# Two empty places in the gate's tick list, and three changes of order at the experts' beginning, in a fused attention and mixture-of-experts kernel

## Chip, cores, metric

The kernel runs on one core of one Trainium2 chip. The metric is the device time of one execution in microseconds (us). Every launch computes everything from the inputs in DRAM to the output in DRAM.

## The reference

Three stages follow each other: attention that keeps the 32 largest scores of a row, a gated linear layer, and a layer of eight experts of which each token uses one.

```python
scores = scale * q @ k.T                       # 4 batches, 8 heads, 576 x 576, head size 64
kth = np.partition(scores, -32)[..., -32]      # per row
attn = softmax(where(scores >= kth, scores, -1e9)) @ v
x = attn.transpose(0, 2, 1, 3).reshape(2304, 512)
x = ((x @ w_a) * (x @ w_b)) @ w_out            # 512 -> 1536 -> 512, weights in float64
xn, en = x / norm(x), expert_emb / norm(expert_emb)
logits = xn @ en.T / tau
e = argmax(logits); g = softmax(logits)[e]
out = g * (relu(x @ w1[e]) @ w2[e])            # 512 -> 1024 -> 512, per token
```

All products are made of three float32r products of high and low parts, so that each input of a product is first split: high = rounded value, low = value - high.

## The kernel before

**Attention.** 144 blocks of 128 rows, one per step. A step's work goes through the engines in this order: TensorE makes two score halves (L373), ScalarE copies them out (L374, tile `s`, 5 buffers), VectorE finds the 32nd largest value with four MAX8 and three MATCH_REPLACE8 (L394, L397) and writes a bias (L399), ScalarE makes a penalty (L406, tile `z`), GpSimd subtracts it (L409), ScalarE takes the exponential with its row sum (L411), TensorE turns the block (L428). After the last block of a part, GpSimd adds a small number to the row sums (L437, tile `rc`) and VectorE takes their reciprocal (L439) in the middle of its top-k work. In this stage the order of TensorE, VectorE, ScalarE and GpSimd is that in which the Python code issues the instructions. Each engine executes its own list in order.

**Gated layer in the background.** `moe1` is a generator. It works on 9 groups of 256 tokens; each has 12 blocks f of 128 hidden columns. `background` advances it between the attention's instructions, one `yield` at a time. For a block f TensorE makes the two products a and b (24 matmuls, L729), ScalarE copies them out (L743, tile `gab`, 2 buffers), GpSimd multiplies them (`gab<-gab`), ScalarE makes the high part (`gh`), GpSimd the low part (`gl<-gab,gh`). Two blocks later (`LAG` = 2) TensorE uses `gl` and `gh` for the second product (`second`, L676). The three small operations are not issued at once: they are entries of a list `pend`, from which `tick()` takes one at a time (all three then show as L663, the line of `tick`). A block has seven ticks: three in the a product, two in the b product, two in `second`. Before, the list of a block is: product, empty, high part, low part. `second(f)` empties what is left of f's entries before it issues its matmuls. When attention has ended (about 836 us), the remaining groups run alone; the routing of tokens to experts is made beside them.

**Experts.** From here only TensorE's order is that of the code; the other engines' orders come from a scheduler. `first_expert` does 256 rows of one expert early, `last_tile` its last 80 rows, and the loop over e = 1..7 the other experts. The rows are gathered by GpSimd's indirect DMA (`pick`, L1132), turned by TensorE (`turn_x`, L1145) and split by ScalarE (L1148) and VectorE (L1149) into `xT`. Weights come in units of 1 MB (`raw`, 2 buffers, L1093), and each unit is split into `u` (4 buffers) in two halves: ScalarE L1099, VectorE L1100, some 1.05 and 1.22 us for a half. `upto(n)` issues units up to n. A `gate` is a ScalarE copy of one column (L1096) that writes into the unit's first half and reads a tile named by `gate[0]`: that half can't be converted before that tile is written. In `last_tile` L1288 are the matmuls of the first product, L1291 its ReLU, L1295 the turning of its result, L1298 and L1299 its split into `hT`, L1181 the second product. In the loop `stage1` is the first product (L1169, ReLU L1173, low part L1174), and L1342 the second.

Of the kernel before, what the change touches and what calls it, by code (L numbers as in the profile page):

```python
# [87 lines left out]
def fused_kernel(  # L88
# [25 lines left out]
    NE, _, F2 = w1.shape  # L114
# [3 lines left out]
    NF2 = F2 // P  # L118
# [88 lines left out]
    with ExitStack() as ph:  # L207
# [440 lines left out]
        def moe1(G):  # L648

            gi = G.gi  # L650
            g0, N = GROUPS[gi]
            G.inputs()
            xg, ws = G.xg, G.ws
            LA = WB // 2 - 1
            while len(ws) < LA:
                G.load()
            px = [None, None]
            gs = {}
            pend = []

            def tick():
                if pend:
                    pend.pop(0)[1]()  # L663

            def second(f, tiles=(0, 1)):
                while pend and pend[0][0] <= f:
                    tick()
                hi, lo = gs[f]
                if gi == 0:
                    conv.need(2, f)  # L670
                for t in tiles:
                    ts = slice(t * P, (t + 1) * P)
                    if f == 0:
                        px[t] = mp.tile([P, DM], F32, name="x1", bufs=2)
                    for i, (g, w) in enumerate(((lo, 0), (hi, 1), (hi, 0))):
                        pe.matmul(  # L676
                            px[t], g[:, ts], wo[:, w, f], start=(f == 0 and i == 0), stop=(f == NF - 1 and i == 2)
                        )
                    if f == NF - 1:
                        r = route(g0 // P + t, px[t])  # L680
                        next(r)
                        routes.append(r)
                        debt[1] = 0.0
                    tick()
                    yield 0.64

            begun = {}
            if gi == 0:
                for f in range(2):
                    while not (conv.ready(0, f) and conv.ready(1, f)):  # L690
                        yield None
                    begun[f] = [mp.tile([P, 512], F32, name=nm, bufs=2)[:, :256] for nm in ("ab", "x1")]
                    for i in range(2):
                        wt = conv.tiles[i, f]
                        for c in range(KC - 1):
                            for a, x in TERMS1:
                                pe.matmul(
                                    begun[f][i],
                                    wt[:, a, c, :],
                                    xg[x][:, c, :],  # L700
                                    start=(c == 0 and (a, x) == TERMS1[0]),
                                    stop=False,
                                )
                            yield 3 * N / 2400
                while ready[0] < N:
                    yield None

            for f in range(NF):
                nxt = todo[1][1] if len(todo) > 1 and todo[1][0] <= now[0] else None
                if f >= (NF - 4 if gi else NF - 1) and nxt:  # L710
                    nxt.inputs()
                if f + LA < NF:
                    G.load()
                elif nxt:
                    nxt.load()
                if gi == 0:
                    conv.begun = f
                    while now[0] < NRW and not (conv.ready(0, f) and conv.ready(1, f)):
                        yield None
                    for i in range(2):  # L720
                        conv.need(i, f)
                    ws[f] = [conv.tiles[i, f] for i in range(2)]
                ab = mk.tile([P, 2, GN], F32, name="gab")
                p = None if f in begun else mp.tile([P, 2, 256], F32, name="ab", bufs=2)
                ps_ = begun[f] if f in begun else [p[:, 0], p[:, 1]]
                for i, wt in enumerate(ws[f]):
                    terms = [(a, x, c) for (a, x) in TERMS1 for c in range(KC) if f not in begun or c == KC - 1]
                    for j, (a, x, c) in enumerate(terms):
                        pe.matmul(  # L729
                            ps_[i],  # L730
                            wt[:, a, c, :],
                            xg[x][:, c, :],
                            start=(j == 0 and f not in begun),
                            stop=(j == len(terms) - 1),
                        )
                        if j % 4 == 3 and (i == 0 or j < 11):
                            tick()
                            yield 4 * N / 2400
                if f in begun:
                    for i in range(2):  # L740
                        act.activation(ab[:, i], ps_[i], AF.Copy)
                else:
                    act.activation(ab, p, AF.Copy)  # L743
                recent[0] = ab
                yield 4 * N / 2400
                hi = mk.tile([P, GN], F32R, name="gh", bufs=LAG + 2)
                lo = mk.tile([P, GN], F32R, name="gl", bufs=LAG + 2)
                gs[f] = hi, lo
                pend.append((f, partial(pool.tensor_tensor, ab[:, 0], ab[:, 0], ab[:, 1], op=OP.mult)))
                pend.append((f, lambda: None))  # L750
                pend.append((f, partial(act.activation, hi, ab[:, 0], AF.Copy)))
                pend.append((f, partial(pool.tensor_tensor, lo, ab[:, 0], hi.bitcast(F32), op=OP.subtract)))
                if f >= LAG:
                    yield from second(f - LAG)
            tail[0] = tail[0] if gi == len(GROUPS) - 1 else lambda: None
            nxt = todo[1] if len(todo) > 1 and todo[1][0] <= now[0] and todo[1][1].ws else None
            if nxt:
                nxt[2] = moe1(nxt[1])
            for tiles in ((0,), (1,)) if gi == len(GROUPS) - 1 else ((0, 1),):
                for f in range(NF - LAG, NF):  # L760
                    for _ in range(6 if nxt else 0):
                        yield next(nxt[2])
                    for _ in range(NTF if tiles[0] >= ET else 0):
                        tail[0]()
                    yield from second(f, tiles)
# [307 lines left out]
    with ExitStack() as ph:  # L1073
        w2p = ph.enter_context(tc.tile_pool(name="w2p", bufs=2, side="right"))

        gate = [None]
# [194 lines left out]
        def last_tile():  # L1271
# [5 lines left out]
            pick(xs[t], ids[0][:m, t, 0:1])  # L1277
            nx = gather(NE - 1)
            turn_x((xs, xT), t)
            turn_x(nx, 0, NE - 1)  # L1280
            hs = []
            for half in range(2):
                u = units[half]
                p = bank("h")
                n = 0
                for a, b in TERMS:
                    for c in range(KC):
                        pe.matmul(p[:m], xT[b][:, c, t * P :], u[:, a, c, :], start=(n == 0), stop=(n == 11))  # L1288
                        n += 1
                hs.append(result())  # L1290
                act.activation(hs[-1][:m], p[:m], AF.Relu)  # L1291
            for half, h in enumerate(hs):
                pt = bank("tr")
                for j in range(4):
                    pe.transpose(pt[:, j * P : j * P + m], h[:m, j * P : (j + 1) * P], ident[:m, :m])  # L1295
                pv = pt.rearrange("p (j k) -> p j k", j=4)[:, :, :m]
                hi, lo = (y[:, half * 4 : half * 4 + 4] for y in hT)
                act.activation(hi, pv, AF.Copy)  # L1298
                dve.tensor_tensor(lo, pv, hi.bitcast(F32), op=OP.subtract)  # L1299
# [18 lines left out]
        for e in range(1, NE):  # L1318
            r = NE - e
            n, M = caps[r], rows_of(r)  # L1320
            nx = None
# [11 lines left out]
            if e + 1 < NE:  # L1333
                yT = wx.tile([P, KC, cap], F32, name="yT", bufs=1)[:, :, :n]
                for d in range(KC):
                    p = bank("y")[:, :n]
                    for f in range(NF2):
                        if f % 4 == 0 and d == 0:
                            upto(4 * e + 2 + f // 4 + UB)
                        u = units[4 * e + 2 + f // 4]  # L1340
                        for i, (a, b) in enumerate(TERMS):
                            pe.matmul(  # L1342
                                p,
                                u[:, b, f % 4, d * P : (d + 1) * P],
                                hT[a][:, f],
                                start=(f == 0 and i == 0),
                                stop=(f == NF2 - 1 and i == 2),
                            )
                        if f == XF and d:
                            turn_x(nx, d - 1, r - 1)  # L1350
# [95 lines left out]
```

## Time and profile before

| what | value |
|---|---|
| median of 3 runs (lowest, highest) | 1262.11 us (1260.44, 1264.21) |
| the profiled execution | 1259.81 us |
| its span, first to last instruction | 1258.0 us |
| TensorE matmul busy, share of the span | 1139.1 us, 91% |
| VectorE | 917.0 us, 73% |
| ScalarE | 819.5 us, 65% |
| GpSimd | 728.4 us, 58% |
| DMA, mean | 190 GB/s |
| mean granted TensorE clock | 0.967 of 2.4 GHz |

The sums are made against the profiled execution's own time; it lies 2.3 us (0.2%) below the median of the three runs. In the rows further down, "busy" is time in which an engine executed, a number in square brackets is the engine's idle time just before the instruction and the name behind the arrow is what ended it. PEld is TensorE's weight load, which runs beside the matmuls. An engine name with q (POOLq) is its sequencer.

### The profile page before, as it was taken

How to read it: one execution, taken by the hardware profiler on the slowest of the kernel's cores; microseconds unless marked ns; L12 is line 12 of the kernel's file. 1: busy time of each engine (PE TensorE's matmuls, PEld its weight loads, DVE VectorE, ACT ScalarE, POOL GpSimd, SP SyncE). 2: the span in 40 equal slices, each digit the busy share in tenths (PEclk: the TensorE clock that was granted, in tenths of full speed). 3: DMA queues.
4: the chain of work that ended last, by engine and by line, in shares of the span. 5: the costliest groups of instructions: out<-in, count | busy, mean ns of one | idle time of the engine just before them, and what ended most of it. 6: DMA issues, size and time to landing. Idle time of an engine off the chain costs nothing. (4 is left out here: it accounts for less than half of the span.)

```text
span 1258.0 us, 23887 instructions
## 1 busy us (share of the span) xinstructions
PE 1139.1 (91%) x8124; PEld 983.9 (78%) x8125; DVE 917.0 (73%) x2015; ACT 819.5 (65%) x1964; POOL 728.4 (58%) x1195
## 2 busy tenths in 40 slices
PE   5676789988999998999999998989999989999996
PEld 4445567777887887888887887777898868999995
DVE  8999999999999998899999988850110215655540
ACT  5777988887877877777877877653542424545441
POOL 5565787776777876676787776664555420232221
PEclk8788999999999998999999999999999989999999
DMA  7334667666774666667565677656997235465530
GB/s 235 129 113 139 200 213 254 221 214 199 250 226 139 193 208 214 183 202 212 179 189 181 209 198 208 199 146 206 336 288 220 97 123 205 170 209 207 193 101 27
DMA packets 129200, 240.05 MB, mean 191 GB/s; under 512 B 24896, under 2 KB 74176, under 8 KB 129074
## 3 DMA queue, kind: packets, MB, share of 16 engines
q1 hardware_dynamic: 125170, 228.74, 57.6%
q0 software_dynamic: 3904, 9.75, 2.0%
q8 instruction: 65, 1.06, 0.3%
q14 instruction: 61, 0.50, 0.1%
HBM read 198.38 MB, written 40.31 MB: 190 GB/s over the span
## 5 line engine op out<-in xcount | busy, mean ns | idle before, releaser
L394 DVE MAX8 t<-y 128x8 f32<-128x576 f32 x432 | 311.7, 749 | 2.7
L409 POOL TENSOR_TENSOR z<-s,z 128x576 f32<-128x576 f32 x144 | 206.2, 1432 | 49.7 <-ACT z L406 44.3
L397 DVE MATCH_REPLACE8 y<-t,y 128x576 f32<-128x576 f32 x288 | 213.9, 743 | 0.0
L729 PE MATMUL ab<-xg,wab 128*128 128x256 f32 x1398 | 210.5, 290 | 2.2 <-DMA wab<-wab_d 0.9
L729 PEld LDWEIGHTS ab<-xg,wab 128*128 128x128 f32 x1398 | 183.8, 191 | 5.2 <-DMA wab<-wab_d 1.1
L428 PE MATMUL tr<-ident,z 128*128 128x128 f32 x720 | 135.2, 287 | 51.5 <-ACT z L411 47.2
L729 PE MATMUL ab<-raw,wab 128*128 128x256 f32 x1152 | 172.6, 288 | 3.8 <-DMA wab<-wab_d 2.6
L374 ACT ACTIVATE s<-tr 128x288 f32<-128x288 f32 x288 | 118.3, 411 | 72.3 <-POOL z L409 37.3
L729 PEld LDWEIGHTS ab<-raw,wab 128*128 128x128 f32 x1152 | 150.3, 189 | 6.9 <-DMA wab<-wab_d 2.6
L431 ACT ACTIVATE wt<-tr 128x384 f32<-128x384 f32 (+2 forms) x320 | 128.1, 413 | 41.4 <-PE tr L428 40.7
L428 PEld LDWEIGHTS tr<-ident,z 128*128 128x128 f32 x720 | 89.2, 145 | 71.8 <-ACT z L411 60.3
L676 PE MATMUL x<-wo,gh 128*128 128x512 f32 x432 | 136.7, 398 | 0.0
L663 POOL TENSOR_TENSOR gab<-gab 128x256 f32<-128x256 f32 x108 | 81.1, 751 | 90.0 <-ACT gab L743 79.7
L1153 POOL DMA_INDIRECT out_dram<-o,ids x24 | 31.2, 1300 | 174.1 <-ACT o L1152 122.2
L1100 DVE TENSOR_TENSOR u<-raw,u 128x1024 fp32r<-128x1024 f32 x64 | 75.9, 1221 | 73.1 <-ACT u L1099 50.1
L373 PE MATMUL tr<-kT,qT 128*128 128x288 f32 x512 | 123.6, 326 | 4.6 <-ACT s L374 3.5
L663 POOL TENSOR_TENSOR gl<-gab,gh 128x256 fp32r<-128x256 f32 x108 | 83.0, 768 | 59.5 <-ACT gh L663 50.8
L411 ACT ACTIVATE z<-z,bi 128x576 f32<-128x576 f32 x144 | 112.2, 779 | 0.3 <-POOL z L409 0.3
L406 ACT ACTIVATE z<-s,bi 128x576 f32<-128x576 f32 x144 | 111.4, 773 | 0.2 <-DVE bi L399 0.2
L394 DVE MAX8 t<-s 128x8 f32<-128x576 f32 x144 | 107.0, 743 | 5.0 <-ACT s L374 4.8
L397 DVE MATCH_REPLACE8 y<-t,s 128x576 f32<-128x576 f32 x144 | 106.9, 742 | 0.0
L676 PE MATMUL x<-wo,gl 128*128 128x512 f32 x216 | 93.3, 432 | 6.3 <-POOL gl L663 6.2
(201 smaller groups left out, 2240.2 us busy)
## 6 DMA issues: line engine op xcount, KB each, us to landing
wab<-wab_d SPq DMA_DIRECT2D x192, 512.0 KB, 4.5
raw<-in_moe_w_dram SPq DMA_DIRECT2D x28, 1024.0 KB, 5.3
wab_d<-wab SPq DMA_DIRECT2D x24, 512.0 KB, 4.5
kT<-kT_d SPq DMA_DIRECT2D x20, 576.0 KB, 5.8
vs<-in_v_dram SPq DMA_DIRECT2D x36, 256.0 KB, 3.1
kT_d<-kT SPq DMA_DIRECT2D x16, 576.0 KB, 5.0
raw<-in_moe_w_a_dram SPq DMA_DIRECT2D x12, 512.0 KB, 4.4
raw<-in_moe_w_b_dram SPq DMA_DIRECT2D x12, 512.0 KB, 4.3
```

Source lines behind the costliest of these rows:

```text
L373: pe.matmul(p, l, r, start=(i == 0), stop=(i == len(terms) - 1))
L374: act.activation(t.s[:, cs], p, AF.Copy, scale=SCALE)
L394: dve.max(v, cur)
L397: dve.match_replace(out=rest, in_to_replace=v, in_values=cur, imm_value=LOWEST)
L406: act.activation(t.w, t.s, AF.Relu, bias=t.bi[:, 1:2], scale=-HUGE)
L409: pool.tensor_tensor(t.w, t.s, t.w, op=OP.subtract)
L411: act.activation(t.w, t.w, AF.Exp, bias=t.bi[:, 0:1], accum_out=t.o.sm[:, t.slot : t.slot + 1])
L428: pe.transpose(pt[:, i * P : (i + 1) * P], t.w[:, k0 : k0 + P], ident)
L431: act.activation(th[:, sl, w], pv[:, :, src], AF.Copy)
L663: pend.pop(0)[1]()
L676: pe.matmul(px[t], g[:, ts], wo[:, w, f], start=(f == 0 and i == 0), stop=(f == NF - 1 and i == 2))
L729: pe.matmul(ps_[i], wt[:, a, c, :], xg[x][:, c, :], start=(j == 0 and f not in begun), stop=(j == len(terms) - 1),)
```

## The change

Two empty entries are added to the list of a block's small operations: one ahead of the product, one ahead of the low part. The list now has six entries for the block's seven ticks: empty, product, empty, high, empty, low. So the product and the high part are issued one tick later, the low part two ticks later. In `last_tile` the turning of the next expert's first 128 gathered rows is issued behind the first product's matmuls rather than ahead of them. In the loop, a gate is put on the unit that is issued at the start of the second product: its first half waits for the last block of `hT`.

```diff
@@ moe1
                 gs[f] = hi, lo
+                pend.append((f, lambda: None))
                 pend.append((f, partial(pool.tensor_tensor, ab[:, 0], ab[:, 0], ab[:, 1], op=OP.mult)))
                 pend.append((f, lambda: None))
                 pend.append((f, partial(act.activation, hi, ab[:, 0], AF.Copy)))
+                pend.append((f, lambda: None))
                 pend.append((f, partial(pool.tensor_tensor, lo, ab[:, 0], hi.bitcast(F32), op=OP.subtract)))
@@ last_tile
             nx = gather(NE - 1)
             turn_x((xs, xT), t)
-            turn_x(nx, 0, NE - 1)
             hs = []
             for half in range(2):
                 u = units[half]
...
                 hs.append(result())
                 act.activation(hs[-1][:m], p[:m], AF.Relu)
+            turn_x(nx, 0, NE - 1)
             for half, h in enumerate(hs):
@@ the loop over e
                     for f in range(NF2):
                         if f % 4 == 0 and d == 0:
+                            gate[0] = hT[0][:, NF2 - 1, 0:1] if f == 0 else None
                             upto(4 * e + 2 + f // 4 + UB)
```

What this moves, first on GpSimd in the attention stage, around the `rc` of a part that ends near 371 us. Before:

```order
L663 TENSOR_TENSOR gab<-gab 128x256
L408 TENSOR_SCALAR bi<-t_4627 128x1
L409 TENSOR_TENSOR z<-s,z 128x576
L663 TENSOR_TENSOR gl<-gab,gh 128x256
L663 TENSOR_TENSOR gab<-gab 128x256
L408 TENSOR_SCALAR bi<-t_4722 128x1
L409 TENSOR_TENSOR z<-s,z 128x576
L437 TENSOR_SCALAR rc<-sm 128x5
```

and with the change:

```order
L408 TENSOR_SCALAR bi<-t_4626 128x1
L409 TENSOR_TENSOR z<-s,z 128x576
L663 TENSOR_TENSOR gab<-gab 128x256
L663 TENSOR_TENSOR gl<-gab,gh 128x256
L408 TENSOR_SCALAR bi<-t_4722 128x1
L409 TENSOR_TENSOR z<-s,z 128x576
L437 TENSOR_SCALAR rc<-sm 128x5
L663 TENSOR_TENSOR gab<-gab 128x256
```

Each of the two gate products has moved behind the softmax subtraction that followed it, the second one behind the `rc` too. TensorE's and VectorE's orders are the same in the whole attention stage; on ScalarE only the high parts (and a routing instruction) stand later.

Second, TensorE at the experts' beginning (`xT` 80x512 are the 80 last rows of the first expert, `tr<-ident,xg 128x128` the next expert's rows). Before:

```order
L1145 MATMUL tr<-ident,xg 128x80 x4
L1145 MATMUL tr<-ident,xg 128x128 x4
L1288 MATMUL h<-u,xT_14069 80x512 x4
L1288 MATMUL h<-u,xT_14070 80x512 x4
L1288 MATMUL h<-u,xT_14069 80x512 x8
L1288 MATMUL h<-u,xT_14070 80x512 x4
L1288 MATMUL h<-u,xT_14069 80x512 x4
L1295 MATMUL tr<-ident,o 128x80 x8
```

and with the change:

```order
L1147 MATMUL tr<-ident,xg 128x80 x4
L1289 MATMUL h<-u,xT_14069 80x512 x4
L1289 MATMUL h<-u,xT_14070 80x512 x4
L1289 MATMUL h<-u,xT_14069 80x512 x8
L1289 MATMUL h<-u,xT_14070 80x512 x4
L1289 MATMUL h<-u,xT_14069 80x512 x4
L1147 MATMUL tr<-ident,xg 128x128 x4
L1297 MATMUL tr<-ident,o 128x80 x8
```

The four transposes of the next expert's rows have moved behind all 24 matmuls (the changed kernel's line numbers are one to three higher).

Third, ScalarE in the second expert (e = 1), from its first product to its second (`hT` are the ReLUs, `u<-raw 128x1024` halves of weight units). Before:

```order
L1173 ACTIVATE hT_14199<-h 128x264
L1099 ACTIVATE u<-raw 128x1024 x2
L1173 ACTIVATE hT_14199<-h 128x264 x2
L1099 ACTIVATE u<-raw 128x1024 x2
L1173 ACTIVATE hT_14199<-h 128x264 x3
L1099 ACTIVATE u<-raw 128x1024 x2
L1173 ACTIVATE hT_14199<-h 128x264 x2
L1099 ACTIVATE u<-raw 128x1024 x2
```

and with the change:

```order
L1175 ACTIVATE hT_14199<-h 128x264
L1101 ACTIVATE u<-raw 128x1024 x2
L1175 ACTIVATE hT_14199<-h 128x264 x2
L1101 ACTIVATE u<-raw 128x1024 x2
L1175 ACTIVATE hT_14199<-h 128x264 x4
L1101 ACTIVATE u<-raw 128x1024 x2
L1175 ACTIVATE hT_14199<-h 128x264
L1098 ACTIVATE u<-hT_14199 128x1
L1101 ACTIVATE u<-raw 128x1024 x2
```

The seventh ReLU has moved ahead of a unit's two conversions, the eighth still stands behind them, and the gate's copy stands in front of the last two.

## Rows read from the trace of the kernel before

**Rows 1.** Busy time by stretch, with the columns in the first line

```profile
core 0: us, PE busy (x) PEld busy (x) DVE busy (x) ACT busy (x) POOL busy (x), PEclk, DMA share, GB/s
...
200.00:836.00 636.00, 600.26 (x4557) 514.38 (x4556) 592.79 (x1362) 492.12 (x1274) 462.78 (x798) 0.98 0.66 202
...
1024.50:1030.50 6.00, 5.97 (x16) 3.92 (x17) 0.69 (x1) 0.60 (x1) 1.08 (x2) 0.50 0.67 248
1030.50:1041.50 11.00, 10.24 (x53) 6.69 (x52) 6.49 (x8) 6.62 (x11) 0.41 (x1) 0.99 0.16 53
...
1100.00:1258.00 158.00, 147.63 (x1023) 142.34 (x1022) 71.26 (x102) 64.25 (x102) 35.94 (x30) 0.98 0.43 147
```

**Rows 2.** Waits in attention, 200 to 836 us: total us, times, longest

```profile
POOL gab L663 <- ACT gab L743: 55.2, 43, 3.9
...
POOL gl L663 <- ACT gh L663: 36.6, 35, 4.0
...
DVE rc L439 <- POOL rc L437: 25.8, 11, 3.7
...
PE x L676 <- POOL gl L663: 6.2, 3, 3.8
...
PE tr L316 <- POOL qs L229: 5.5, 2, 3.2
...
DVE t L394 <- ACT s L374: 4.0, 2, 2.9
```

**Rows 3.** GpSimd's timeline ahead of two late rc: start us, us, instruction

```profile
368.55 0.74 POOL L663 TENSOR_TENSOR gab<-gab 128x256 f32<-128x256 f32 x1 [2.31 <-ACT gab L743]
...
369.43 1.43 POOL L409 TENSOR_TENSOR z<-s,z 128x576 f32<-128x576 f32 x1
370.94 0.25 POOL L437 TENSOR_SCALAR rc<-sm 128x5 f32<-128x5 f32 x1
...
808.31 0.74 POOL L663 TENSOR_TENSOR gab<-gab 128x256 f32<-128x256 f32 x1 [1.33 <-ACT gab L743]
```

**Rows 4.** VectorE's timeline at three late reciprocals

```profile
322.84 0.18 DVE L439 RECIPROCAL rc<-rc 128x4 f32<-128x4 f32 x1 [2.44 <-POOL rc L437]
...
371.22 0.19 DVE L439 RECIPROCAL rc<-rc 128x5 f32<-128x5 f32 x1 [2.14 <-POOL rc L437]
...
810.97 0.18 DVE L439 RECIPROCAL rc<-rc 128x4 f32<-128x4 f32 x1 [2.26 <-POOL rc L437]
```

**Rows 5.** TensorE and GpSimd at the ends of two groups

```profile
259.72 0.50 PE L676 MATMUL x<-wo,gl 128*128 128x512 f32 x1 [2.10 <-POOL gl L663]
...
259.63 0.40 POOL L227 TENSOR_SCALAR qs<-qr 128x256 fp32r<-128x256 f32 x1
...
478.46 0.80 PE L676 MATMUL x<-wo,gl 128*128 128x512 f32 x1 [3.85 <-POOL gl L663]
```

**Rows 6.** Timeline of the experts' beginning

```profile
1019.88 0.47 PE L1145 MATMUL tr<-ident,xg 80*128 80x80 f32 x4 [0.16 <-DMA xg<-row_d,ids]
...
1020.53 0.44 ACT L1148 ACTIVATE xT<-tr 128x320 fp32r<-128x320 f32 x1
...
1024.53 1.12 PE L1145 MATMUL tr<-ident,xg 128*128 128x128 f32 x4 [4.18 <-DMA xg<-row_d,ids]
...
1025.30 8.23 PE L1288 MATMUL h<-u,xT 128*80 128x512 f32 x24
...
1030.56 2.49 PEld L1288 LDWEIGHTS h<-u,xT 128*80 128x80 f32 x11 [0.18 <-issue]
...
1035.06 0.92 PE L1181 MATMUL y<-u,hT 128*80 128x512 f32 x3 [0.35 <-DVE hT L1299]
```

**Rows 7.** DMA issues, 1017.60 to 1017.95 us: KB each, us to landing

```profile
raw<-in_moe_w_dram SPq DMA_DIRECT2D x1, 1024.0 KB, 5.3
```

**Rows 8.** Timeline in expert e = 1, from first to second product

```profile
1053.92 2.01 ACT L1099 ACTIVATE u<-raw 128x1024 fp32r<-128x1024 f32 x2 [3.00 <-DMA raw<-in_moe_w_dram]
...
1057.77 2.87 PE L1342 MATMUL y<-hT,u 128*128 128x264 f32 x12 [2.20 <-DVE hT L1174]
```

## The prediction

> **What bounds the kernel now.** I read the busy times by stretch, the waits of the attention stage, and then timelines. Over the whole span TensorE is the busiest engine (91%, in the table above), but the two places that the change touches have limits of their own. In attention (200 to 836 us) TensorE is busy for 600.3 and VectorE for 592.8 of 636 us, GpSimd for 462.8 [rows 1]: two engines run nearly full, each with some 40 us of idle time, and neither has much room to wait. The reader should see in the waits that VectorE's are nearly all of one kind: its reciprocal waits 25.8 us, in 11 pieces, for the `rc` that GpSimd makes; for scores, its real input, it waits 4.0 us [rows 2]. GpSimd in turn stands 55.2 us in front of a gate product and 36.6 us in front of a low part, since ScalarE has not made their inputs yet [rows 2]. The two belong together: at 368.55 GpSimd had stood 2.31 us for a gate product, worked 0.74 us on it, and only then came to the softmax subtraction (1.43) and `rc` at 370.94 [rows 3]; VectorE, at its reciprocal, had waited 2.14 us [rows 4].
>
> At the experts' beginning the bound is one gather. TensorE finishes the transposes of the last 80 rows at 1020.35 (1019.88 + 0.47), and then stands 4.18 us for the next expert's rows, although the 24 matmuls that follow need only the copy that ScalarE ends at 1020.97 (1020.53 + 0.44) [rows 6]. The idle time has a second price: from 1024.5 to 1030.5 the granted clock is 0.50, that is 1.2 GHz [rows 1], so the 24 matmuls take 8.23 us, though the last 11 take only 2.49 [rows 6]. From 1100 us on TensorE is busy for 147.6 of 158 us [rows 1], what is missing being the drain at the very end; a gain here is kept.
>
> **The change, part by part.**
>
> *Gate list.* No instruction is added; an empty entry costs nothing on the chip. Matched one by one, the changed order puts 38 of the 72 gate products of this stretch, and 46 of the 72 low parts, behind at least one other GpSimd instruction. GpSimd's idle time just before these 84, from whatever cause, sums to 38.0 + 31.6 = 69.6 us (the two rows have 91.8 for all 144 [rows 2]); the others keep their place. What this saves counts only where VectorE or TensorE stood for GpSimd. Ten `rc` waits are long (2 to 3.7 us, one 0.89). Ahead of seven of them, from the one at 322.84 us to the one at 810.97 [rows 4], a gate operation that stood in front of `rc` now stands behind it. Near 371 us its wait and work are 2.31 + 0.74 = 3.05 us [rows 3], more than the 2.14 that VectorE lost [rows 4]. At 811 us a product (1.33 + 0.74) [rows 3] leaves, and a low part before it, and all 2.26 can go. Counted so for the seven, each capped by VectorE's wait and by how long the subtraction's own input had been there, it makes 0.9 + 2.1 + 1.7 + 0.9 + 2.0 + 1.9 + 2.3 = 11.8 us, the upper bound. The lower bound is a loss: low parts are issued two ticks later. In the middle of a group they are finished 3 to 25 us before TensorE wants them, in most places over 6. But at group ends TensorE already stands for them, 6.2 us in 3 places [rows 2], 2.10 and 3.85 of it in the two longest [rows 5]. At the first of these the changed order puts one small split (0.40) [rows 5] in front of the low part, at the second nothing. Six group ends at 0.5 us make +3 us. Between -11.8 and +3 I take **-7**, some 60% of the upper bound: VectorE runs only 3 us or so behind its scores, so an advance is soon limited by TensorE. That TensorE can follow in part is seen in its own waits for GpSimd, such as 5.5 us for split queries in two places [rows 2]; at one of them a gate product that stood in front leaves.
>
> One rule speaks against that term. The Trainium skill, "Perfetto Trace Analysis", section "Identifying the Most-Contended Engine", says to improve the engine of highest occupancy first; GpSimd is only third here. By that rule the term would be 0 and not -7. The rows side with it on TensorE's occupancy and against it on the waits; it is a rival below.
>
> *Transposes behind the matmuls.* The matmuls can start at about 1021.05, some 0.1 us after ScalarE's copy. Per matmul 2.49 / 11 = 0.226 us at 2.4 GHz [rows 6], so 24 take 5.5 and end at 1026.5. The clock should hold, for the gap is now 0.7 us; the gaps of under 0.5 us between 1030.5 and 1041.5 leave it at 0.99 [rows 1]. The gathered rows have landed by 1024.53, so the four transposes follow at once (0.6) and cover the ReLU of the second half. After them a new chain appears: the second half's transposes use the PSUM bank that the moved ones filled, so they wait for its ScalarE copy (0.60) and VectorE split (0.69), and then for their own copy and split (0.44 and 0.49). The second product then starts near 1029.1 where it started at 1035.06 [rows 6]: **-5.9**. The weight unit that ScalarE splits between the two ReLUs is no obstacle: its load landed 5.3 us after its issue at 1017.7 [rows 7], at 1023.0. Bounds: -6.5 if that chain hides, -3.2 if the clock falls all the same (13 matmuls at 0.2 us more).
>
> *The gate in the loop.* Before, TensorE stands 2.20 us in expert e = 1 for the seventh and eighth block of `hT`, whose ReLUs are behind two conversions on ScalarE that waited 3.00 us for a weight load [rows 8]. With the change the seventh goes ahead, but the eighth still stands behind them, so the wait moves three matmuls back and stays. The load is issued when an earlier unit has been split, and that advances by 5.4 us where TensorE advances by 5.9. What is left is three matmuls fewer at half clock, 0.7, less that 0.5: **-0.2**; bounds +1 and -3.7 (the wait and the slow matmuls behind it all gone). In the other experts the eighth ReLU stood ahead of the gated half already; a copy of 0.2 us each on ScalarE, which is under half busy there [rows 1], costs nothing.
>
> Sum: -7.0 - 5.9 - 0.2 = -13.1 us. On the profiled execution's 1259.8 that is 1246.7; the median of the runs stood 2.3 higher, so the forecast is **1249**.
>
> **Rivals.**
>
> *Attention gives nothing (B).* TensorE is the bound there: the reciprocals come sooner, VectorE then waits for scores instead, and the attention ends when it did. For it: TensorE's 94%, and waits for GpSimd that only change place. Against it: VectorE waits only 4.0 us for scores now [rows 2]. Time: 1262.1 - 6.1 = 1256.
>
> *The beginning gives only a third (C).* The new chain through the PSUM bank, or the gathers, take most of it: -7 - 2 = 1253.
>
> *Little change (D).* The shifted order costs attention 3 to 5 us through high and low parts that come just late, and offsets the experts' gain: 1259 to 1262.
>
> *Slower (E).* At a group's end the last block's low part is now issued only when `second` empties the list, right in front of its matmuls and behind six steps of the next group; TensorE then stands there every time. At six group ends with the longest wait seen, 3.85 [rows 5], it is 23.1 - 6.2 = +16.9, with the experts' -6.1 and nothing else 1273. It decides from 2.7 us a group end on ((6.1 + 3.8 + 6.2) / 6). Against it: at these six ends the low part is moved behind 1, 4, 0, 2, 0 and 1 GpSimd instructions only.
>
> **How the numbers follow.** The forecast has 0.55, B 0.22, C 0.10, D 0.06, E 0.07. A measurement of this kernel tells 0.3%, 3.8 us, from no change. Faster: 0.53 of the forecast, 0.19 of B, 0.09 of C, in all 0.81; same 0.12 (D whole, the edges of the others); slower 0.07 (E). The forecast's own range, attention -3 to -12 and the experts -5 to -6.5, is 1243.6 to 1254; with B and C, and a little beyond at the low end for attention at its bound, the range is 1241 to 1259.
>
> **What would show it.** Right: VectorE's wait for `rc` falls from 25.8 to some 14 us, GpSimd's two waits to some 40; the last reciprocals come about 7 us sooner; L1289 starts within 1 us of the 80-row transposes, at 2.4 GHz; the next second product starts 8 to 9 us after those transposes, not 14.7. Wrong: an attention stage of the same length with VectorE's waits for scores grown (B), a wait of over 2 us in front of the moved transposes or of L1297 (C), or TensorE's waits for `gl` well over 6.2 us (E).

## The result and the profile after

| | before | changed |
|---|---|---|
| median (runs, lowest to highest) | 1262.82 us (6, 1260.44 to 1264.21) | 1250.90 us (6, 1249.34 to 1253.81) |
| ratio | | 0.9911, 95% interval 0.9891 to 0.9931 |
| the profiled execution | 1259.81 us | 1249.34 us |
| its span | 1258.0 us | 1247.5 us |

The change saves 11.9 us, 0.9%. The forecast was 1249, the range 1241 to 1259. The total came out, but not the way it was summed: one of its two large terms was right, and the other is almost absent.

The attention stage first. Its waits, 200 to 836 us, in the changed kernel (total us, times, longest; to be read against [rows 2]):

```profile
POOL z L409 <- ACT z L406: 36.0, 36, 3.2
...
POOL gl L663 <- ACT gh L663: 31.0, 37, 1.9
POOL gab L663 <- ACT gab L743: 30.0, 28, 3.9
...
DVE m L795 <- ACT lg L791: 16.2, 6, 3.5
DVE rc L439 <- POOL rc L437: 15.2, 8, 5.0
ACT s L374 <- POOL z L409: 14.8, 12, 3.2
...
DVE t L394 <- ACT s L374: 7.1, 6, 2.4
PE x L676 <- POOL gl L663: 6.6, 2, 4.8
```

Two more rows of the same view before, which the readings below need:

```profile
ACT s L374 <- POOL z L409: 36.6, 30, 2.8
...
POOL z L409 <- ACT z L406: 15.2, 16, 2.3
```

GpSimd's wait for a gate product fell from 55.2 to 30.0 us and its wait for a low part from 36.6 to 31.0, but its wait for ScalarE's penalty, which the softmax subtraction needs, grew from 15.2 to 36.0. ScalarE's copy of the scores (L374) has to wait until the subtraction (L409) has read the `s` buffer that it is to fill; that wait fell from 36.6 to 14.8. VectorE's wait for `rc` fell from 25.8 to 15.2, and TensorE's for `gl` stayed (6.2, now 6.6). But VectorE's other waits grew, for scores from 4.0 to 7.1 and for the routing's logits (`m<-lg`) from 10.1 to 16.2. Of the 10.6 us that it no longer waits for `rc`, 9.2 came back inside this window. The windows are the same 636 us long, and in the changed kernel more of the work lies inside (TensorE 603.53 us busy, before 600.26 [rows 1]):

```profile
200.00:836.00 636.00, 603.53 (x4587) 518.59 (x4588) 593.25 (x1370) 498.22 (x1283) 465.47 (x803) 0.98 0.66 204
```

The last reciprocal of the attention starts at 849.15 us, where it started at 855.23; the last second product of the gated layer ends 7.3 us sooner (988.47, before 995.77). Of the 10.5 us between the two profiled spans, 7.6 lie ahead of the 80-row transposes (1012.26, before 1019.88) and 2.9 behind them.

Then the experts' beginning, TensorE, ScalarE and GpSimd (start us, us, instruction; in brackets the idle time before it and what ended it; against [rows 6]):

```profile
1012.26 0.44 PE L1147 MATMUL tr<-ident,xg 80*128 80x80 f32 x4
1013.72 5.74 PE L1289 MATMUL h<-u,xT 128*80 128x512 f32 x24 [1.02 <-ACT xT L1150]
1019.30 0.60 PE L1147 MATMUL tr<-ident,xg 128*128 128x128 f32 x4
1019.74 0.44 PE L1297 MATMUL tr<-ident,o 80*128 80x80 f32 x4
1024.10 0.80 PE L1297 MATMUL tr<-ident,o 80*128 80x80 f32 x4 [3.92 <-DVE xT L1151]
1024.62 1.55 PE L1183 MATMUL y<-u,hT 128*80 128x512 f32 x3
...
1016.74 0.59 ACT L1292 ACTIVATE o<-h 80x512 f32<-80x512 f32 x1 [3.08 <-PE h L1289]
1017.23 1.05 ACT L1101 ACTIVATE u<-raw 128x1024 fp32r<-128x1024 f32 x1
1022.24 0.59 ACT L1292 ACTIVATE o<-h 80x512 f32<-80x512 f32 x1 [3.96 <-DMA out_dram<-o,ids]
1022.73 0.58 ACT L1150 ACTIVATE xT<-tr 128x512 fp32r<-128x512 f32 x1
...
1014.73 0.95 POOL L1134 DMA_INDIRECT xg<-row_d,ids  x1 [0.30 <-issue]
1015.98 1.04 POOL L1155 DMA_INDIRECT out_dram<-o,ids  x1 [0.30 <-issue]
```

Up to 1019.7 it is as forecast: L1289 starts 1.02 us behind the 80-row transposes and takes 5.74 us at 2.4 GHz, and the moved transposes follow at once. Then TensorE stands 3.92 us between the two halves of L1297. The release is VectorE's split of the moved rows, but the chain does not begin there: ScalarE's second ReLU (L1292), which stands ahead of the moved rows' copy in ScalarE's order, waited 3.96 us for a DMA. It writes into an output tile `o`, of which there are three; the one whose turn it is still holds the first early result of this expert, whose scatter to DRAM GpSimd issued only at 1015.98, behind six gathers. And the wait has the old second price, 1.2 GHz behind it:

```profile
1024.10:1028.00 3.90, 3.90 (x14) 2.92 (x15) 2.25 (x4) 3.04 (x5) 0.00 (x0) 0.50 0.14 55
```

So the second product starts 12.4 us after the start of the 80-row transposes, 11.9 us after their end; from that end 8 to 9 had been forecast. In the profiled execution of before it was 15.2 and 14.7. Below, all such times count from the start.

### The profile page after: what moved, and what is told of

Same layout as the page of the kernel before. It is cut to its first block, busy times and chain, and to the rows that moved or that the text cites. A ratio compares the mean times of both kernels' runs of the same rounds, so it can differ in the third digit from the quotient of the medians.

```text
span 1247.5 us, 23919 instructions
## 1 busy us (share of the span) xinstructions
PE 1134.9 (91%) x8124; PEld 982.7 (79%) x8125; DVE 914.2 (73%) x2015; ACT 822.5 (66%) x1970; POOL 731.1 (59%) x1195
## 5 line engine op out<-in xcount | busy, mean ns | idle before, releaser
L409 POOL TENSOR_TENSOR z<-s,z 128x576 f32<-128x576 f32 x144 | 206.2, 1432 | 73.0 <-ACT z L406 70.3
L374 ACT ACTIVATE s<-tr 128x288 f32<-128x288 f32 x288 | 117.8, 410 | 58.4 <-PE tr L373 35.1
L373 PEld LDWEIGHTS tr<-kT,qT 128*128 128x128 f32 x512 | 87.5, 202 | 18.2 <-ACT s L374 5.7
```

Of the source, the lines that this page charges most:

```text
L373: pe.matmul(p, l, r, start=(i == 0), stop=(i == len(terms) - 1))
L374: act.activation(t.s[:, cs], p, AF.Copy, scale=SCALE)
L409: pool.tensor_tensor(t.w, t.s, t.w, op=OP.subtract)
```

## The experiments

Every kernel below was timed against the kernel before on the same chip. The kernel before had medians of 1261.15 to 1261.65 us in these runs; single executions of one kernel lie as far apart as 10 us and more, so differences come from the ratios, and 0.2% is 2.5 us. "Before" and "changed" name the kernel that is edited.

**1. Each part alone.** The two empty entries:

```diff
 (before)
+                pend.append((f, lambda: None))
                 pend.append((f, partial(pool.tensor_tensor, ab[:, 0], ab[:, 0], ab[:, 1], op=OP.mult)))
...
+                pend.append((f, lambda: None))
                 pend.append((f, partial(pool.tensor_tensor, lo, ab[:, 0], hi.bitcast(F32), op=OP.subtract)))
```

> The kernel before with the two empty entries alone, nothing changed at the experts' beginning. Theory (the sum of the prediction, with the attention term as the changed kernel's trace reads it): the last reciprocal comes 6 us sooner, the last second product of the gated layer 7 us sooner, and the whole time falls by 6 to 8 us from before, to about 1255.5; TensorE still stands some 4 us for the next expert's rows and runs the 24 matmuls behind it at half clock. Rival B (attention gives nothing that lasts, all of the gain comes from the experts): within 2 us of before. Rival (the attention's gain is larger than its trace shows, since the three edits hinder one another): 9 us or more.

Measured 1252.77 us, ratio 0.9935 (0.9914 to 0.9955): -8.2 us, between -10.8 and -5.7. The time is as the theory has it and rival B falls: the attention's gain lasts to the end. (A gain of 9 us or more, the other rival, is within the interval.) The signs in its profiled execution are weaker than expected: the last reciprocal starts at 853.82 us, 1.4 sooner than before rather than 6, and the last second product of the gated layer ends at 992.04, 3.7 sooner rather than 7. One execution is a poor measure here. The 80-row transposes start at 1019.9, 1025.2, 1022.5 and 1021.1 us in the four traces without the entries and with nothing else changed in attention (before, gate alone, transposes alone, and transposes with their own tile, below), and at 1015.8, 1012.3 and 1015.9 in the three with both entries; the means are 7.5 us apart.

The moved transposes:

```diff
 (before)
-            turn_x(nx, 0, NE - 1)
             hs = []
...
+            turn_x(nx, 0, NE - 1)
             for half, h in enumerate(hs):
```

> The kernel before with the moved transposes alone. Theory (a new wait takes the gain): the second ReLU of the last 80 rows writes into an output tile whose scatter to DRAM is still under way, so the ReLU waits about 4 us, TensorE stands about 4 us between the two halves of L1295, and the second product behind it starts at half clock; the whole time falls by only 0 to 2 us. The prediction's own term: TensorE never stands over 1 us there, and the time falls by 5 to 6.5 us. Rival C's chain through the PSUM bank: a fall of about 2 us too, but with the ReLU on time and the wait in front of the moved transposes or behind their split.

Measured 1260.07 us, ratio 0.9997 (0.9980 to 1.0015): -0.4 us, between -2.5 and +1.9. The prediction's -5.9 lies outside. ScalarE's and TensorE's rows are those of the changed kernel again:

```profile
1032.76 0.59 ACT L1290 ACTIVATE o<-h 80x512 f32<-80x512 f32 x1 [3.94 <-DMA out_dram<-o,ids]
...
1034.62 0.79 PE L1295 MATMUL tr<-ident,o 80*128 80x80 f32 x4 [4.24 <-DVE xT L1149]
```

The gate in the loop:

```diff
 (before)
                         if f % 4 == 0 and d == 0:
+                            gate[0] = hT[0][:, NF2 - 1, 0:1] if f == 0 else None
                             upto(4 * e + 2 + f // 4 + UB)
```

> The kernel before with the loop's gate alone. The trace of the changed kernel shows the wait in expert e = 1 down from 2.20 to 1.53 us and no matmul at half clock behind it, some 1.8 us in all. Theory (the gate itself does that): the time falls by 1.5 to 2.5 us, and the matmuls behind the wait run at full clock. Rival (the prediction's term, -0.2; the rest was a matter of how the earlier shifts moved the weight load against TensorE): within 0.7 us of before, with some 2 us of wait and half clock behind it left.

Measured 1260.69 us, ratio 0.9994 (0.9975 to 1.0014): -0.8 us, between -3.2 and +1.8. The interval contains both -0.2 and -1.8, but the trace decides. The wait in expert e = 1 is still there with the gate alone, in front of all 12 matmuls of two blocks; with the transposes alone it is in front of 9, as in the changed kernel. Gate alone, transposes alone, and the two entries alone:

```profile
1060.38 1.73 PE L1343 MATMUL y<-hT,u 128*128 128x264 f32 x12 [2.48 <-DVE hT L1174]
```

```profile
1059.34 1.37 PE L1342 MATMUL y<-hT,u 128*128 128x264 f32 x9 [1.38 <-DVE hT L1174]
```

```profile
1051.60 1.74 PE L1344 MATMUL y<-hT,u 128*128 128x264 f32 x12 [2.16 <-DVE hT L1176]
```

So it is the moved transposes that put the seventh ReLU ahead of the conversions, and the gate does nothing that can be seen. Nor was the half clock behind this wait (2.87 us for 12 matmuls [rows 8]) a property of the kernel: with the entries alone nothing is changed there, and the 12 take 1.74.

**2. The scatter.** The second ReLU gets memory that is free at that time:

```diff
 (changed)
-                hs.append(result())
+                o = wx.tile([P, KC, cap], F32, name="yT", bufs=1) if half else None
+                hs.append(o.rearrange("p c j -> p (c j)")[:, :DM] if half else result())
                 act.activation(hs[-1][:m], p[:m], AF.Relu)
```

> The changed kernel, with the second ReLU of the last 80 rows written into a tile of its own (the memory of the later yT, not in use there) in place of an output tile whose scatter is under way. Theory (that scatter is what takes back the gain of the moved transposes): the ReLU comes about 4 us sooner, the wait of 3.92 us in front of the second half of L1297 falls below 1 us, the second product starts at full clock, and the time falls by 3.5 to 5.5 us from the changed kernel, to about 1246. Rival (the PSUM bank and the split of the moved rows take it anyway): the wait stays over 2 us and the time falls by less than 1 us. Rival (the weight units are late next): the second product starts sooner, but TensorE then stands the same 4 us for a unit, and the time falls by 1 us or less.

Measured 1250.34 us, ratio 0.9909 (0.9879 to 0.9939), the same as the changed kernel within the intervals (0.9909 / 0.9911 = 0.9998; -0.3 us, between -4.8 and +4.3). Theory had 3.5 to 5.5 us; no gain and a wait of over 2 us is what the rival had. The wait in front of the second half of L1297 fell from 3.92 to 2.21 us only, though no scatter is waited for any more. What is late in this execution is the first ReLU. The last matmul that it needs ends near 1020.2 (halfway through L1289, which starts at 1017.32 and takes 5.74), and it starts at 1022.53; the profile shows no instruction that released it:

```profile
1022.53 0.59 ACT L1293 ACTIVATE o<-h 80x512 f32<-80x512 f32 x1 [5.26 <-remote]
...
1025.99 0.50 PE L1298 MATMUL tr<-ident,yT 80*128 80x80 f32 x4 [2.21 <-DVE xT L1151]
```

The same edit on the kernel before:

```diff
 (before)
-            turn_x(nx, 0, NE - 1)
             hs = []
...
-                hs.append(result())
+                o = wx.tile([P, KC, cap], F32, name="yT", bufs=1) if half else None
+                hs.append(o.rearrange("p c j -> p (c j)")[:, :DM] if half else result())
...
+            turn_x(nx, 0, NE - 1)
             for half, h in enumerate(hs):
```

> The kernel before with the moved transposes and with the second ReLU's own tile, nothing else. Theory (by the stretches of the traces): from the 80-row transposes to the end it takes 232.7 us, where the unchanged beginning takes 233.8 to 238.1 (it differs from execution to execution with the landing of the gathers) and the moved transposes alone 235.1; so the time falls by 1 to 4 us from before. Rival (the prediction's term holds once the scatter is out of the way): 5 to 6.5 us. Rival (the moved transposes are worth nothing even so): within 1 us of before.

Measured 1254.87 us, ratio 0.9943 (0.9929 to 0.9956): -7.2 us, between -9.0 and -5.6. That is more than the theory allowed, and nearer to the prediction's term. No ReLU is late here, the wait is 1.18 us, and the second product starts 9.5 us after the 80-row transposes (1021.06) at full clock (granted clock 1.00 from 1030.15 to 1033):

```profile
1028.53 0.44 PE L1296 MATMUL tr<-ident,o 80*128 80x80 f32 x4
1030.15 0.50 PE L1296 MATMUL tr<-ident,yT 80*128 80x80 f32 x4 [1.18 <-DVE xT L1149]
1030.55 0.92 PE L1181 MATMUL y<-u,hT 128*80 128x512 f32 x3
```

With the same transposes moved and nothing else, the kernel gained 0.4. The two differ by the tile alone, so on the kernel before it is shown that the scatter took the gain: with it out of the way the move is worth 5.6 to 9.0 us. On the changed kernel the same tile gave nothing that can be told (-0.3 us, above), and why the timed runs differ so is open. How much of the 7.2 lies in this stretch is less sure, too. In all profiled executions the time from the start of e = 2 to the end is the same within 0.4 us, so the stretches before it can be compared (us, worked out from starts in the timelines):

| kernel | wait for gathered rows | 80-row transposes to second product | to e = 1 | to the end of the span |
|---|---|---|---|---|
| before | 4.18 | 15.2 | 21.7 | 238.1 |
| entries alone | 3.33 | 13.1 | 19.6 | 234.5 |
| gate alone | 2.41 | 12.2 | 18.7 | 233.8 |
| transposes alone | none | 12.7 | 21.1 | 235.1 |
| changed | none | 12.4 | 21.1 | 235.2 |
| changed, own tile | none | 10.5 | 18.6 | 232.6 |
| before, transposes and own tile | none | 9.5 | 16.0 | 231.3 |

Two things are to be seen. The first three rows execute the same instructions up to e = 1 and still differ there by 3.0 us, to the end by 4.3; the gathered rows land at different times. The traces of experiments 3 and 4 have three more executions of this beginning on the kernel before (waits of 3.44, 3.62 and 2.17 us for the rows; 234.6, 234.9 and 233.8 us to the end). The profiled execution of before, from which the prediction worked, is the slowest of these six, and the middle of the six is 234.6. And the five executions with the transposes moved but without the tile (three of them from experiments 4 and 5) take 234.3 to 235.4 us to the end, the three with both (one from experiment 6) 231.3 to 232.6. So in this stretch the move with the scatter in its way is worth nothing that can be told, and with the tile 2 to 3 us against the middle of the six. That is less than the 7.2 of the timed runs; the rest is not placed. Nor is all kept that is won up to e = 1: in the last row TensorE waits 2.66 us for `hT` there, with the transposes alone 1.38, and of 5.1 us between these two rows 3.8 are left at the end.

**3. What in the gate list helps.** The entry ahead of the product alone, and the one ahead of the low part alone (one of the two lines of the first diff each).

> The kernel before with the empty entry ahead of the gate product alone. Theory (the gain is VectorE's wait for rc, and it is the product that stood in front of rc): at five of the long waits (near 323, 371, 523, 736 and 811 us) the product moves behind rc already with this entry, as it does with both; the rc waits fall from 28.8 to some 19 us in the whole span, and the time falls by 6 to 8 us from before, as with both entries. Rival (the low part is what counts): a fall of 2 us or less. Rival (each entry gives its half): some 4 us.

> The kernel before with the empty entry ahead of the low part alone. Theory (as for the product's entry): of the five long rc waits only the one near 736 us has a low part moved from its front, so the rc waits stay above 24 us and the time falls by 2 us or less. Rival (the low part is what counts): a fall of 5 us or more. Rival E (low parts late at a group's end cost TensorE): slower than before by 1 us or more, with TensorE's waits for gl well over 6.6 us.

The product's entry: 1253.06 us, ratio 0.9943 (0.9914 to 0.9973), -7.2 us, between -10.8 and -3.4. The low part's: 1255.31 us, 0.9951 (0.9932 to 0.9970), -6.2 us, between -8.6 and -3.8. As measured, either entry gives most of what both give; half of it each, 4.1 us, lies just inside both intervals. For the product's entry the time is as expected, but `rc` waits in the whole span fell only from 28.7 to 23.4 us where 19 had been expected. For the low part's the theory falls: it should have given 2 us or less. In its trace VectorE's wait for `rc` hardly moved (25.8 before, now 23.2), while GpSimd's for the low part halved (36.6 to 17.6) and ScalarE's for the softmax subtraction, which has to have read an `s` buffer before the next scores are copied into it, fell from 36.6 to 27.6 (GpSimd's wait for the gate product grew, from 55.2 to 63.4):

```profile
POOL gab L663 <- ACT gab L743: 63.4, 44, 3.9
...
ACT s L374 <- POOL z L409: 27.6, 23, 2.8
DVE rc L439 <- POOL rc L437: 23.2, 11, 5.2
...
POOL gl L663 <- ACT gh L663: 17.6, 23, 1.9
```

So what an empty entry buys is not `rc` alone. The rows fit that whatever stands behind a waiting gate operation on GpSimd comes sooner, the subtraction of the next block too, and with it a free `s` buffer; no run takes that wait away by itself, so its share of the 6.2 us is argued and not shown.

**4. The wait for rc taken away.** VectorE takes the reciprocal of the sums itself; the added 1e-9 is left out.

```diff
 (before, and changed)
-                pool.tensor_scalar(o.rc[:, sl], o.sm[:, sl], 1e-9, None, op0=OP.add)
...
-            dve.reciprocal(o.rc[:, sl], o.rc[:, sl])
+            dve.reciprocal(o.rc[:, sl], o.sm[:, sl])
```

> The kernel before with its tick list unchanged, and without GpSimd's rc: VectorE takes the reciprocal of the row sums directly (the added 1e-9 is left out; the sums are at least 1). Theory (VectorE's wait for rc is what the two entries relieve): the 28.8 us of waits are gone, and the time falls by as much as with the two entries or more, 7 to 12 us, though GpSimd's waits in front of the gate product and the low part stay at some 55 and 36 us. Rival (the entries help through GpSimd's other work, the subtraction z that ScalarE waits for): 3 us or less. Rival B (TensorE bounds the attention stage; VectorE then waits for scores): 3 us or less, with VectorE's waits for scores grown from 4 to over 15 us.

> The changed kernel without GpSimd's rc, in the same way. Theory (one and the same wait): 18.9 us of rc waits are left in the changed kernel, with gains that are limited by TensorE, so the time falls by 2 to 5 us from the changed kernel; the two edits overlap, and together they give less than the sum of each alone. Rival (independent gains): a fall of 7 us or more. Rival B (TensorE is the bound by then): within 1.5 us of the changed kernel.

On the kernel before: 1255.24 us, ratio 0.9948 (0.9929 to 0.9968), -6.6 us, a little under the theory's 7 to 12, and over the 3 us that either rival allowed. VectorE no longer waits for GpSimd's `rc`, GpSimd waits in front of the product and the low part somewhat longer than before, and of the 25.8 us 14.7 came back as a wait for scores (4.0, now 18.7). The profiled execution is a slow one, 1259.39 us, 4.2 above the kernel's median, so the 14.7 may be more than is usual:

```profile
POOL gab L662 <- ACT gab L742: 60.9, 44, 3.9
POOL gl L662 <- ACT gh L662: 39.9, 38, 4.0
...
DVE t L394 <- ACT s L374: 18.7, 13, 3.8
```

On the changed kernel: 1250.91 us, ratio 0.9924 (0.9898 to 0.9951), no better than the changed kernel's 0.9911. Its waits for scores are 15.7 us, where the changed kernel has 7.1. Three different edits (either entry, no `rc`) give 6 to 7 us each as measured, and with both entries in, taking `rc` away adds nothing that can be told. Something else sets the end by then.

**5. What sets the end of the attention now.** About equal amounts of work, as reckoned, were added to the changed kernel, on TensorE (a first matmul issued twice) and on VectorE (a MAX8 issued twice):

```diff
 (changed)
+                        if j == 0 and f not in begun and gi < 6:
+                            pe.matmul(ps_[i], wt[:, a, c, :], xg[x][:, c, :], start=True, stop=True)
                         pe.matmul(
```

```diff
 (changed)
                 dve.max(v, cur)
+                if r == 0 and t.n % 5 == 0:
+                    dve.max(v, cur)
```

> The changed kernel with 140 matmuls more on TensorE in the attention stage: the first matmul of each a and b product of the first six groups is issued twice, 140 times 0.157 us, 22.0 us of work. Theory (TensorE is what bounds the attention stage by now, which is why the change without rc gives nothing more): slower than the changed kernel by 15 to 22 us. Rival (VectorE is the bound): slower by under 8 us. Rival (the two in turn, each on the path for about half of it): 8 to 15 us.

> The changed kernel with 29 MAX8 more on VectorE: in every fifth block of the attention the first MAX8 is executed twice, 29 times 0.745 us, 21.6 us of work. Theory (TensorE is the bound by now, VectorE has 7 us of waits for scores and 15 us for rc to give): slower than the changed kernel by under 10 us. Rival (VectorE is the bound): 17 to 22 us. Rival (the two in turn): 10 to 17 us.

TensorE: 1260.92 us, ratio to before 0.9992 (0.9972 to 1.0012). Against the changed kernel that is 0.9992 / 0.9911 = 1.0082, +10.2 us, or 6.7 to 13.8 with the two intervals combined by squares. VectorE: 1252.30 us, 0.9926 (0.9911 to 0.9942), 1.0015 times the changed kernel, +1.9 us, and no difference that can be told. The stretches from the seventh reciprocal to the last, for the changed kernel, with more on TensorE, and with more on VectorE (length, then busy us of PE, PEld, DVE, ACT, POOL, clock, DMA):

```profile
213.80:849.10 635.30, 601.41 (x4597) 517.59 (x4596) 579.61 (x1345) 492.05 (x1273) 459.22 (x801) 0.98 0.65 202
```

```profile
215.40:859.40 644.00, 613.65 (x4727) 529.83 (x4726) 580.91 (x1346) 494.38 (x1273) 460.32 (x801) 0.99 0.65 199
```

```profile
216.30:852.90 636.60, 602.58 (x4602) 517.10 (x4601) 597.42 (x1367) 493.08 (x1275) 460.43 (x801) 0.98 0.65 201
```

Of the 140 added matmuls 130 fall into this stretch. They raised TensorE's busy time by 12.2 us, 0.09 each and not the 0.157 that was reckoned with, and the stretch grew by 8.7, some 70% of that. VectorE's busy time rose by 17.8 us and the stretch by 1.3: it came out of VectorE's waiting. So in the changed kernel TensorE is what mostly bounds the attention, and VectorE's waits are slack. The expected 15 to 22 us was wrong in its price. The 10.2 lie in the range given for the two engines in turn, but by that rival VectorE's work would have cost 10 us or more. The expectation for VectorE held. No work was added on ScalarE or GpSimd.

**6. Together.** The changed kernel with the own tile and without `rc` (the diffs of 2 and 4 joined; 1e-9 left out).

> The changed kernel with the second ReLU's own tile and without GpSimd's rc (the 1e-9 is left out of the row sums). Theory (the experts' 2.6 us are kept to the end, and rc gives nothing more): 2 to 3 us faster than the changed kernel. Rival (both edits give nothing that can be measured): within 1 us of it. Rival (rc and the two entries add up): 6 us or more.

Measured 1247.75 us, ratio 0.9879 (0.9863 to 0.9894): 15.3 us faster than before and 4 faster than the changed kernel (0.9879 / 0.9911 = 0.9968, interval 0.9943 to 0.9993 in the same way). It is the fastest kernel of the study. By themselves neither the tile (0.9909) nor the missing `rc` (0.9924) gave the changed kernel anything that can be told, so the timed runs do not say which of them the 4 us come from. The trace speaks for the tile: from the 80-row transposes to the end it takes 232.6 us, in the changed kernel 235.2.

## Why the prediction was right, and where it was not

**The gate list, -7 (bounds -11.8 to +3).** Measured -8.2 (-10.8 to -5.7): the size is right. The mechanism, GpSimd's idle time ahead of work that others need, is right too, but the prediction measured it by VectorE's `rc` waits alone, seven of them, and took 60% since "an advance is soon limited by TensorE". The wait for `rc` did fall to 15.2, where some 14 was forecast, and the last reciprocal came 6.1 us sooner, where 7 was. GpSimd's two waits, though, were to fall to some 40 us and are 61.0, and its wait for the penalty grew. And the low part's entry gained 6.2 us with that wait almost unchanged. The count gave the right size, but the `rc` waits are not the whole cause. Rival B was half right in its mechanism, since waits for scores and logits took back most of what `rc` gave, and wrong in its result. That TensorE takes over as the limit is shown by the added work: the stretch grew by 8.7 us for 12.2 on TensorE, and by 1.3 for 17.8 on VectorE.

The rule by which this term was put at 0 is that of the Trainium skill, "Perfetto Trace Analysis", section "Identifying the Most-Contended Engine": the engine of highest occupancy first. It did not price the edit: GpSimd is only fourth in occupancy in this stage, not third (73%, behind ScalarE's 77% [rows 1]), and the edit still was worth 8 us. For TensorE, the same section of the Trainium skill judges the headroom by the weight loads' busy time or the share of peak arithmetic, not by the matmuls' busy time. Here the weight loads are busy for 81% and VectorE for 93% [rows 1], while the added work counts on TensorE, so it is not plain that the rule names the limit either.

**The low part at group ends (rival E, +3 in the bounds).** TensorE's wait for `gl` is 6.6 us, before 6.2. The price was nothing.

**The transposes, -5.9 (bounds -6.5 to -3.2).** This is the step that failed: alone they gave -0.4 (-2.5 to +1.9). Two errors stand in it. The step followed ScalarE's second ReLU for its input and for the weight unit in front of it ("no obstacle"), but not for the tile that it writes. The tile's last use was a scatter that GpSimd issues behind six gathers; the first product now ends 7.2 us behind the start of the 80-row transposes (before 13.7), so that scatter became the last thing the ReLU waits for, 3.96 us, and the clock fell again behind it. With a tile of its own the same move gave -7.2 (-9.0 to -5.6) on the kernel before, though only 2 to 3 us of that are found in the stretch. The second error is the base: 4.18 us of wait for gathered rows [rows 6], and a second product 15.2 us behind the transposes, were one execution's; in five others of the same code it was 2.17 to 3.62, and 11.6 to 13.3. The chain itself was sized well: from the end of the 80-row transposes it took 9.0 us with the own tile, where 8.7 had been reckoned. Rival C had the size of the result (a third or less) and named a wait in front of L1297 as its sign, but its chain through the PSUM bank was not the cause: that chain is what is left with the own tile where no ReLU was late, 1.18 us.

**The gate in the loop, -0.2.** Measured -0.8 (-3.2 to +1.8), and no trace of it in the rows. The text put the moved seventh ReLU down to the gate; it comes with the transposes.

**The sum.** -8.2 - 0.4 - 0.8 = -9.4 us for the parts alone, and -11.2 (-13.8 to -8.7) by the ratio for all three: the same within the intervals. The forecast was 1.9 us below the measured median. The attention gave a little more than its term; of the beginning's 5.9 next to nothing arrived.

## What to carry to other kernels

Before moving a step forward, ask of every instruction in its chain what it writes into, and who has still to read the old contents; an output tile that a DMA drains is free when the DMA has landed, and that DMA may be queued behind others. A wait read from one profiled execution is a sample: where it ends with a DMA, look at the same code in several executions before its price enters a sum. And a wait that goes is a gain only as far as the next limit: add a known amount of work to each of two engines, and the one that passes it on is the limit.

## What the runs showed of the hardware

The clock does not follow from the length of a wait alone. In expert e = 1 the 12 matmuls behind a wait of 2.20 us took 2.87 us in the kernel before [rows 8], at a granted clock of 0.53 (1.00 ahead of the wait), and those behind 2.16 and 2.48 us took 1.74 and 1.73, at 1.00, with the entries alone and with the gate alone.

ScalarE's first ReLU of one execution started some 2.3 us after its last input with no releaser in the records (the 5.26 us row above). The same instruction was on time in the other kernels with this edit. It was not explained.
